# Cosine-weighted linear attention and a mixture of adapters: four rows per partition, Q scaling and V cast on GpSimd, routing in threes

## The chip, the cores and the metric

The kernel runs on one core of one Trainium2 chip. The metric is the device time of one execution in microseconds (us), lower is better. Each run is marked fast, or slow when it lies over 1.5% above the fastest of the same kernel. Medians are of all runs; where kernels are compared, fast runs are compared with fast runs.

Some words that come up: PSUM is where the program's matmuls write, SBUF is where its other tiles lie, and an eviction copies a result from PSUM to SBUF. In the profile's lines PE is TensorE, DVE VectorE, ACT ScalarE and POOL GpSimd; SP issues DMAs.

## The reference, cut to what matters

Eight batches, eight heads, 576 positions, 64 features per head. Attention is linear, so K and V of a batch are first summed into one matrix per head. Its output, 4608 rows of 512, goes through a two-of-eight mixture of rank-16 adapters.

```python
def _attn_ref(q, k, v):                       # (8, 8, 576, 64) each
    theta = np.pi / 2.0 * np.arange(S) / S    # by position
    phi = lambda x: np.concatenate([relu(x) * cos(theta), relu(x) * sin(theta)], axis=-1)
    kv  = einsum('bhsf,bhsd->bhfd', phi(k), v)
    z   = sum(phi(k), axis=2)
    return einsum('bhsf,bhfd->bhsd', phi(q), kv) / (einsum('bhsf,bhf->bhs', phi(q), z) + 1e-6)

def _moe_ref(x, w_gate, A, B):                # x (4608, 512)
    logits = x @ w_gate                       # 8 experts, the two best are taken
    # w = softmax of the two best logits
    # x + sum over the two experts of w_e * (x @ A[e]) @ B[e]
```

## The kernel before

Every batch is cut into five groups of rows, four of 128 and one of 64. Each group loads K, Q and V with a DMA each, in rows of 64 floats, which are 256 bytes. K is scaled on ScalarE, V is cast on ScalarE, Q is scaled on VectorE. TensorE sums K times V over the groups. The attention of a group is eight transposes of Q, an eviction, eight products with `kvzsb`, and a division. The adapters follow, group by group, two groups behind.

```python
for gi, (s0, slen) in enumerate(GROUPS):
    nc.sync.dma_start(out=ks[:slen], in_=k[b, :, s0:s0 + slen, :].transpose([1, 0, 2]))
    nc.sync.dma_start(out=qs[:slen], in_=q[b, :, s0:s0 + slen, :].transpose([1, 0, 2]))
    v_eng.dma_start(out=vs[:slen], in_=v[b, :, s0:s0 + slen, :].transpose([1, 0, 2]))
    # ... K scaled on ScalarE (phi), V cast on ScalarE, 8 matmuls into kvz ...
def attention_back(gi):
    phi_op("vector", qp[:slen, :, 0, :], qs[:slen], cos_tab[:slen, gi:gi + 1])   # and sin
    # ... 8 transposes into qpTp, copied by VectorE into qpT, 8 matmuls into nd ...
    nc.vector.reciprocal(rden[:slen], nd_v[:, :, :, D:W])
    nc.vector.tensor_tensor(out=xt[:slen, :], in0=nd_v[:, :, :, 0:D], in1=rd_rep, op=ALU.mult)
def moe_front(gi):
    # ... 4 transposes of xt, xT copied by VectorE, za = xT @ [A | w_gate] ...
    nc.vector.max(out=m8[:slen], in_=logits)
    nc.scalar.activation(eall[:slen], logits, AF.Exp)
    nc.vector.scalar_tensor_tensor(out=em[:slen], in0=logits, scalar=m8[:slen, 1:2],
        in1=eall[:slen], op0=ALU.is_ge, op1=ALU.mult, accum_out=ssum[:slen])
    nc.vector.reciprocal(rs[:slen], ssum[:slen])
def moe_back(gi):
    # zg = za * rs * em (VectorE), zgT by transpose, dx = xt + zgT @ B (TensorE),
    # osb copied from dx by VectorE and ScalarE in turn
    nc.gpsimd.dma_start(out=out[row0:row0 + slen, :], in_=osb[:slen])
for gi in range(NG + 2):
    # attention_back(gi), moe_front(gi - 1), moe_back(gi - 2)
```

The softmax here doesn't subtract the row's maximum and nothing guards it: scores larger than these inputs give would overflow.

## Time and profile before

| | before |
|---|---|
| median of 3 runs | 198.97 us (196.18 to 202.57) |
| span of the profiled run | 198.0 us |
| TensorE / VectorE / ScalarE / GpSimd busy | 130.2 / 141.6 / 97.6 / 28.6 us |
| DMA packets, of them under 512 B | 120,307, 117,856 |

From the page of the kernel before: busy tenths in 40 equal slices of the span, then the packets, then the DMA queues with packets, megabytes and their share of 16 engines' span.

```profile
DVE  0035557991888889486998399768947799999830
DMA  7999999999999999997999999999999921221121
DMA packets 120307, 38.55 MB, mean 195 GB/s; under 512 B 117856, under 2 KB 117856, under 8 KB 120288
q1 hardware_dynamic: 89216, 21.78, 59.9%
q10 hardware_dynamic: 28128, 7.08, 19.3%
q0 software_dynamic: 2944, 9.44, 13.9%
```

The DMA line stays at nine tenths until about four fifths of the span. Nearly all packets are 256-byte rows. The last eight slices have little DMA work left, while VectorE stays busy: a tail.

The stretches view of the kernel before shows the same by the clock. Columns: the stretch, its length, busy time and instruction count of each engine, the granted TensorE clock, the DMA share, GB/s.

```profile
core 0: us, PE busy (x) PEld busy (x) DVE busy (x) ACT busy (x) POOL busy (x), PEclk, DMA share, GB/s
120.00:150.00 30.00, 22.48 (x235) 14.07 (x235) 22.89 (x84) 16.44 (x34) 5.44 (x16) 0.76 1.11 235
160.00:198.00 38.00, 22.07 (x242) 12.61 (x241) 28.72 (x108) 8.44 (x22) 5.48 (x10) 0.85 0.19 67
```

The DMA share is 1.11 in the first of these stretches (over 1 means that the times of the packets add up to more than 16 engines' time), and VectorE works 28.72 of the last 38 us. The groups of instructions below show what VectorE does for each group of rows (count, then busy us and mean ns of one, then idle time before it; the second line is of the full groups alone).

```profile
L85 DVE TENSOR_SCALAR qp<-qs,cos_tab 128x512 bf16<-128x512 f32 (+1 forms) x40 | 18.8, 470 | 2.5 <-DMA qs<-in_q_dram 2.5
L95 DVE COPY qpT<-qpTp 128x1024 bf16<-128x1024 bf16 x32 | 21.9, 683 | 7.8 <-PE qpTp L185 7.4
```

### The profile page before, as it was taken

Reading aid. Unit: us, or ns where it says so; the run is one execution under the profiler, and the core shown is the slowest. Engines: PE = TensorE matmul, PEld = TensorE weight load, DVE = VectorE, ACT = ScalarE, POOL = GpSimd, SP = SyncE. Lnnn points to the kernel's source line nnn. Section 1 sums busy time; section 2 is a strip of 40 time slices with the busy share of each in tenths; the row PEclk is TensorE's granted clock in tenths of the full one; section 3 lists DMA queues with packets and bytes.
Section 4 is the critical chain, followed back from the end, with each engine's and each line's share of the span. In section 5 each row is a group of like instructions: output and inputs, shape, how many; then the busy total and the mean of one; then the engine's idle time right before and its main releaser. Section 6 shows DMA issues by size and latency. Waiting matters only on the chain. (4 is left out here: it accounts for less than half of the span.)

```text
span 198.0 us, 3992 instructions
## 1 busy us (share of the span) xinstructions
PE 130.2 (66%) x1400; PEld 85.7 (43%) x1400; DVE 141.6 (72%) x503; ACT 97.6 (49%) x193; POOL 28.6 (14%) x87
## 2 busy tenths in 40 slices
PE   0036477782866787589875777589768967776560
PEld 0024356441754455346643455356434655343220
DVE  0035557991888889486998399768947799999830
ACT  0865548564374853548464587365555474201110
POOL 1000000320111121112032012211111302121121
PEclk9999999997578969655999589955975589999855
DMA  7999999999999999997999999999999921221121
GB/s 117 196 218 212 198 220 203 194 281 277 242 188 256 225 294 209 238 277 204 207 234 261 224 192 194 280 227 263 178 259 236 238 63 60 103 79 53 56 106 26
DMA packets 120307, 38.55 MB, mean 195 GB/s; under 512 B 117856, under 2 KB 117856, under 8 KB 120288
## 3 DMA queue, kind: packets, MB, share of 16 engines
q1 hardware_dynamic: 89216, 21.78, 59.9%
q10 hardware_dynamic: 28128, 7.08, 19.3%
q0 software_dynamic: 2944, 9.44, 13.9%
q8 instruction: 11, 0.18, 0.4%
q14 instruction: 8, 0.07, 0.1%
HBM read 28.85 MB, written 9.44 MB: 193 GB/s over the span
## 5 line engine op out<-in xcount | busy, mean ns | idle before, releaser
L297 POOL DMA_DIRECT2D out_dram<-osb x40 | 23.0, 575 | 141.7 <-ACT osb L93 53.3
L160 PE MATMUL kvz<-vsb,kp 128*128 128x65 bf16 (+1 forms) x320 | 22.9, 216 | 21.3 <-ACT kp L81 17.1
L185 PE MATMUL qpTp<-ident,qp 128*128 128x128 bf16 (+1 forms) x320 | 32.8, 252 | 5.9 <-DVE qp L85 5.0
L93 ACT CAST vsb<-vs 128x512 bf16<-128x512 f32 (+1 forms) x40 | 24.2, 616 | 22.2 <-DMA vs<-in_v_dram 22.0
L196 PE MATMUL nd<-kvzsb,qpT 128*128 128x65 bf16 (+1 forms) x320 | 20.9, 217 | 15.6 <-ACT kvzsb L93 8.8
L95 DVE COPY qpT<-qpTp 128x1024 bf16<-128x1024 bf16 (+1 forms) x40 | 25.1, 628 | 7.9 <-PE qpTp L185 7.4
L81 ACT ACTIVATE kp<-ks,cos_tab 128x512 bf16<-128x512 f32 (+1 forms) x40 | 28.7, 719 | 3.5 <-DMA ks<-in_k_dram 3.0
L185 PEld LDWEIGHTS <-qp 128*128 128x128 bf16 (+1 forms) x320 | 23.1, 116 | 16.6 <-DVE qp L85 10.4
L81 ACT ACTIVATE kp<-ks,sin_tab 128x512 bf16<-128x512 f32 (+1 forms) x40 | 28.4, 710 | 2.0 <-DMA ks<-in_k_dram 2.0
L160 PEld LDWEIGHTS <-kp 128*128 128x128 bf16 (+1 forms) x320 | 17.4, 112 | 26.9 <-ACT kp L81 19.1
L248 ACT ACTIVATE eall<-za 128x8 f32<-128x8 f32 (+1 forms) x40 | 6.9, 174 | 42.4 <-DVE m_3115 L246 3.7
L211 DVE TENSOR_TENSOR xt<-nd,rden 128x512 bf16<-128x512 f32 (+1 forms) x40 | 27.1, 678 | 0.0
L196 PEld LDWEIGHTS <-qpT 128*128 128x128 bf16 (+1 forms) x320 | 16.5, 115 | 21.3 <-issue 10.8
L284 PE MATMUL dx<-xt,ident 128*128 128x512 bf16 (+1 forms) x40 | 18.9, 473 | 7.2 <-DVE osb L95 4.1
L286 PE MATMUL dx<-Ball,zgT 128*128 128x512 bf16 (+1 forms) x40 | 19.2, 481 | 6.6 <-DVE zgT L95 6.3
L236 PE MATMUL za<-AW,xT 128*128 128x136 bf16 (+1 forms) x160 | 19.2, 252 | 2.0 <-DVE xT L95 1.5
L85 DVE TENSOR_SCALAR qp<-qs,cos_tab 128x512 bf16<-128x512 f32 (+1 forms) x40 | 18.8, 470 | 2.5 <-DMA qs<-in_q_dram 2.5
L93 ACT COPY osb<-dx 128x512 f32<-128x512 f32 (+1 forms) x20 | 11.6, 581 | 17.7 <-PE dx L286 8.9
L95 DVE COPY xT<-mps 128x512 bf16<-128x512 bf16 (+1 forms) x40 | 15.5, 387 | 4.6 <-PE mps L225 4.4
L225 PE MATMUL mps<-ident,xt 128*128 128x128 bf16 (+1 forms) x160 | 18.1, 242 | 1.1 <-DVE xt L211 0.9
L85 DVE TENSOR_SCALAR qp<-qs,sin_tab 128x512 bf16<-128x512 f32 (+1 forms) x40 | 18.6, 465 | 0.0
L95 DVE COPY osb<-dx 128x512 f32<-128x512 f32 (+1 forms) x20 | 13.6, 682 | 5.2 <-PE dx L286 4.9
(225 smaller groups left out, 116.7 us busy)
## 6 DMA issues: line engine op xcount, KB each, us to landing
ks<-in_k_dram SPq DMA_DIRECT2D x32, 256.0 KB, 6.3
qs<-in_q_dram SPq DMA_DIRECT2D x32, 256.0 KB, 6.0
out_dram<-osb POOLq DMA_DIRECT2D x32, 256.0 KB, 4.7
vs<-in_v_dram ACTq DMA_DIRECT2D x24, 256.0 KB, 5.2
vs<-in_v_dram SPq DMA_DIRECT2D x8, 256.0 KB, 6.8
ks<-in_k_dram SPq DMA_DIRECT2D x8, 128.0 KB, 5.5
qs<-in_q_dram SPq DMA_DIRECT2D x8, 128.0 KB, 5.0
out_dram<-osb POOLq DMA_DIRECT2D x8, 128.0 KB, 3.9
```

Source lines behind the costliest of these rows:

```text
L81: nc.scalar.activation(out_ap, in_ap, func, bias=0.0, scale=scale_ap)
L85: eng.tensor_scalar(out=out_ap, in0=in_ap, scalar1=scale_ap, scalar2=0.0, op0=ALU.mult, op1=ALU.max)
L93: nc.scalar.copy(out_ap, in_ap)
L95: getattr(nc, engine).tensor_copy(out_ap, in_ap)
L160: nc.tensor.matmul(out=kvz[:, gg, j * W:(j + 1) * W], lhsT=kp[:slen, h], rhs=vsb[:slen, h, :], start=(gi == 0 and j == 0), stop=(gi == NG ...
L185: nc.tensor.transpose(out=qpTp[:, h, :slen], in_=qp[:slen, h], identity=ident[:slen, :slen],)
L196: nc.tensor.matmul(out=nd[:slen, gg, j * W:(j + 1) * W], lhsT=qpT[:, h, :slen], rhs=kvzsb[:, h, :], start=True, stop=True,)
L211: nc.vector.tensor_tensor(out=xt[:slen, :], in0=nd_v[:, :, :, 0:D], in1=rd_rep, op=ALU.mult,)
L236: nc.tensor.matmul(out=za[:slen, :], lhsT=xT[:, ci, :slen], rhs=AW[:, ci, :], start=(ci == 0), stop=(ci == DCH - 1),)
L284: nc.tensor.matmul(out=dx[:slen], lhsT=ident[:slen, :slen], rhs=xt[:slen, :], start=True, stop=False)
L286: nc.tensor.matmul(out=dx[:slen], lhsT=zgT[:, :slen], rhs=Ball, start=False, stop=True)
L297: nc.gpsimd.dma_start(out=out[row0:row0 + slen, :], in_=osb[:slen])
```

## The change

The intent is fewer, larger packets, less VectorE work and fewer small routing operations. Row s = 4p + j goes to partition p, so four rows of a head are 1 KB in memory, and a batch's K, V or Q comes with one DMA of 1 MB. The last 64 rows of two batches share a tile, which makes 36 full groups out of 40. GpSimd scales Q and casts V; the ReLU of Q moves into VectorE's eviction. Routing runs once per three groups. The loads of K, V and Q and all stores are issued by SP. The K times V sums of the next batch are spread over the groups of this one.

```diff
-    nc.sync.dma_start(out=ks[:slen], in_=k[b, :, s0:s0 + slen, :].transpose([1, 0, 2]))
+    nc.sync.dma_start(out=t, in_=src[b, :, 0:NP * J, :].rearrange("h (p j) d -> p h (j d)", j=J))
 ...
-    copy_op("act", vsb[:slen, :, 0:D], vs[:slen])
+    nc.gpsimd.tensor_copy(vb[:, :, :, 0:D], main["v", b])
 ...
-    phi_op("vector", qp[:slen, :, 0, :], qs[:slen], cos_tab[:slen, gi:gi + 1])
+    nc.gpsimd.tensor_scalar(out=qp[:, :, i, :], in0=src, scalar1=tab[:, j:j + 1],
+                            scalar2=1.0, op0=ALU.mult, op1=ALU.mult)
 ...
-    copy_op("vector", qpT[:, :, :slen], qpTp[:, :, :slen])
+    nc.vector.tensor_scalar_max(qT, qTp, 0.0)
 ...
-    # per group: max, exp, em (fused, with its sum), rs, zg (fused)
+    # per three groups: 3 max, exp, ge, em = ge * ea, ss, rs, wg = em * rs, zg = za * wg
+    nc.vector.tensor_tensor(out=em, in0=ge, in1=ea, op=ALU.mult)
+    nc.vector.tensor_tensor(out=wg, in0=em, in1=rs.to_broadcast([NP, TRI, E]), op=ALU.mult)
 ...
-    nc.gpsimd.dma_start(out=out[row0:row0 + slen, :], in_=osb[:slen])
+    nc.sync.dma_start(out=dst[:, j, :], in_=osb)      # osb always copied by ScalarE
 ...
-    for gi in range(NG + 2): attention_back(gi); moe_front(gi - 1); moe_back(gi - 2)
+    for u in range(G + 2 * TRI + 1):                  # G = 36
+        k_until(need); q_phi(u); attn(u); k_until(frac)   # k_until: K, V of later batches
+        moe_front(u - 1)
+        if u % TRI == 0: route(u // TRI - 1)
+        finish(u - TRI - 1)
```

## The prediction

> **What bounds the kernel now.** For four fifths of the run, the DMA engines. The page's slices show DMA at nine tenths or more from about 5 to 155 us; the stretches view gives a DMA share of 1.06 to 1.12 between 30 and 150 us. The queue part says why: 117,856 of 120,307 packets are under 512 B (a load row is 64 floats, 256 B). The two hardware queues hold 79.2% of 16 engines' 198 us with 117,344 packets: about 21 ns per packet. VectorE (141.6 us busy) and TensorE (130.2 us) are not saturated then (77% and 73% between 100 and 150 us). After the loads a tail of about 40 us is paced by VectorE: 28.7 of 38 us busy, about 4.4 us per group.
>
> **DMA after.** 512 of 576 rows come in 24,576 packets of 1 KB. [...] Estimates:[...] 12,288 remainder packets at 21 ns = 16 us; stores as now, 13.9% of 198 = 27 us[...]. Sum 113 us instead of about 155. Stores now wait in the SP queue in order with the loads; loads stay about a batch ahead, so I expect little loss.
>
> **VectorE after.** Removed: Q scaling, 37.4 us (80 x 468 ns), and its half of the output evictions, 13.6 us. The ReLU rides in the 1024-wide eviction, 683 ns like the copy. Per full group: 683 + reciprocal 202 + xt 679 + xT 414 = 1.98 us. Routing three groups: about 12 small operations of 150 to 200 ns, zg and the zT copy, some 2.4 us, 0.8 a group. 36 x 2.8 = 100 us. [...]
>
> **ScalarE:** 72 x 715 ns K scaling + 36 x 581 ns evictions + 8 x 588 ns + exps = 83 us.
>
> **GpSimd:** the trace's affine select (128x128, 294 ns) against its memset (128x8, 168 ns) gives about 1.05 ns per element; so 0.7 us for 512 elements, 2.3 us for a V cast: 72 x 0.7 + 8 x 2.3 + 4 x 0.7 = 72 us, an estimate; at twice that it becomes the limit.
>
> **TensorE:** eight transposes take 0.62 us at full clock; about 2 us a group, 75 us, more at a lower clock.
>
> **Critical path.** First K and V arrive as 1 MB each behind the remainders, and K scaling of a batch is 5.7 us: the first attention group starts at about 15 us. Then 36 groups with single-buffered transposes, numerators (the second buffer mostly holds K^T V), za and dx, on in-order engines: about 3.4 us a group (VectorE 80 to 85% busy), 122 us. Final routing and stores: 7 us. Sum 145 us. The limit moves from DMA to a VectorE-centred chain; most of the tail disappears.
>
> Predicted 145 us, 130 to 165. Faster by over 2%: 0.95; within 2%: 0.03; slower: 0.02.
>
> **Right if:** DMA share below 0.9 for most of the run, packets under 512 B near 16,000, GpSimd 60 to 100 us busy, VectorE about 100 us and above 70% of the span, tail under 12 us.
>
> **Wrong if:** GpSimd's scaling takes over 1.3 us each (then GpSimd paces, 160 us and up);[...] stores in the SP queue delay loads; or routing chains stop TensorE[...] and a group costs over 4 us.

Passages that no trace or run of this case shows are cut from it: the time of one 1 KB packet and the DMA term worked out from it, the term for the weights, a wait of VectorE's routing products (in two places), and a clause on the clock. The DMA sum came to 113 us with the two cut terms in it; the terms that are left make 43 us. The 145 us of the critical path loses no term (15 + 122 + 7).

## More of the kernel before

The program states data flow only. When it is built, a scheduler puts the instructions of each engine in one fixed order, and an engine then takes them in that order (in the trace of the change, all 1,324 matmuls, 267 VectorE and 98 GpSimd instructions stand in the built order).

## The result, and the profile after

The change takes 167.4 us (median of 4 runs, 165.15 to 168.39), beside 199.93 us for the kernel before in the same rounds (196.18 to 202.57). The ratio is 0.839, with a 95% interval of 0.81 to 0.868. Ratios are computed as the mean time of one kernel's fast runs over that of the other's fast runs of the same rounds, so they are not quite the ratio of the medians. Results are correct. The profiled run took 168.36 us and counts as slow; the fast ones took 166.44 and 165.15 us at almost the same clock (0.867 and 0.874, against 0.86), and e2_bufs4, which has the same built order (see below), has a fast profile with the same five pauses (7.2 to 13.6 us), so this profile may be read.

The direction is as predicted. The time is 22 us above the predicted 145 and 2 us above the top of the range. Of the prediction's own tests, GpSimd's 67.0 us, VectorE's 93.5 us and the 18,400 small packets come out about as stated. Three do not: the DMA share is 0.91 to 1.14 in every 20 us up to 100 us ("below 0.9 for most of the run"), VectorE is busy 56% of the span ("above 70%"), and the tail after the last `xt` takes 16.7 us ("under 12").

From the page after (first line: busy us and share of the span):

```profile
PE 105.9 (64%) x1324; PEld 78.1 (47%) x1324; DVE 93.5 (56%) x267; ACT 74.4 (45%) x132; POOL 67.0 (40%) x98
DVE  0020065696355988857358728966388369892500
PEclk9999999995987999969569659999597599996955
DMA  5999999996799999948998899569992112221332
DMA packets 47727, 38.50 MB, mean 231 GB/s; under 512 B 18400, under 2 KB 42976, under 8 KB 47712
q1 hardware_dynamic: 42880, 37.75, 75.6%
```

Packets under 512 B fell from 117,856 to 18,400. VectorE is busy 93.5 us, 56% of the span. No engine is busy for more than 64% of the span, and the DMA engines run out of full slices at about three quarters. The stretches view after, columns as before:

```profile
40.00:60.00 20.00, 14.22 (x182) 9.91 (x179) 12.63 (x37) 14.13 (x25) 12.49 (x17) 0.88 0.92 266
80.00:100.00 20.00, 17.00 (x211) 12.72 (x209) 11.43 (x30) 10.95 (x20) 9.14 (x12) 0.68 0.96 291
150.00:167.00 17.00, 7.67 (x38) 3.36 (x37) 3.56 (x14) 3.70 (x7) 0.00 (x0) 0.62 0.27 93
```

VectorE works 12.63 and 11.43 of 20 us in the middle, when the prediction had it 80 to 85% busy. The groups that answer to those shown of before:

```profile
L209 POOL TENSOR_SCALAR qp<-qf,cos_tab 128x512 bf16<-128x512 f32 x32 | 22.1, 692 | 13.3 <-DMA qf<-in_q_dram 7.3
L221 DVE TENSOR_SCALAR qT<-qTp 128x1024 bf16<-128x1024 bf16 x36 | 24.5, 681 | 15.1 <-PE qTp L219 14.9
```

The two Q scalings of a group are now 692 ns each on GpSimd. VectorE pays 681 ns for the eviction with the ReLU, where the 1024-wide copy alone had cost 683 ns.

So the work is as small as expected, but it does not flow. The starts of the 36 `xt` products (one per group, in the timeline of VectorE) come in bursts about 2.3 us apart (median) with five pauses: 13.7 us from 35.8 to 49.5, 10.3 from 70.9, 8.7 from 89.3, 8.5 from 106.6 and 8.9 from 123.6. What happens in the third pause? First the timeline of TensorE after (start us, duration us, engine, line, operation, output and inputs; in brackets the idle time before it and what ended it):

```profile
89.30 0.61 PE L219 MATMUL qTp<-ident,qp 128*128 128x128 bf16 x8
90.85 0.61 PE L219 MATMUL qTp<-ident,qp 128*128 128x128 bf16 x8 [0.53 <-POOL qp L209]
92.59 0.91 PE L219 MATMUL qTp<-ident,qp 128*128 128x128 bf16 x8 [1.14 <-DVE qT L221]
93.52 0.50 PE L292 MATMUL zTp<-ident,zg 128*128 128x128 bf16 x3
94.55 0.58 PE L250 MATMUL xTp<-ident,xt 128*128 128x128 bf16 x4 [0.53 <-DVE zT L294]
94.93 0.63 PE L304 MATMUL dx<-Ball,zT 128*128 128x512 bf16 x1
95.65 0.63 PE L258 MATMUL za<-AW,xT 128*128 128x136 bf16 x4
96.23 0.59 PE L303 MATMUL dx<-xt,ident 128*128 128x512 bf16 x1
96.61 0.65 PE L182 MATMUL kvz<-vb_140,kp 128*128 128x65 bf16 x8
97.07 0.63 PE L227 MATMUL nd<-kvs,qT 128*128 128x65 bf16 x8
```

And VectorE in the same stretch:

```profile
89.89 0.31 DVE L266 MAX8 m_1464<-za 128x8 f32<-128x8 f32 x3
90.12 0.67 DVE L221 TENSOR_SCALAR qT<-qTp 128x1024 bf16<-128x1024 bf16 x1
...
92.91 0.56 DVE L284 TENSOR_TENSOR zg<-za,wg 128x384 bf16<-128x384 f32 x1
...
97.74 0.21 DVE L236 RECIPROCAL rden<-nd 128x8 f32<-128x8 f32 x1 [2.14 <-PE nd L227]
```

At 89.89 the routing of three groups starts with its maxima. TensorE has three groups' Q transposes in its order (89.30, 90.85, 92.59), and then the gate transposes `zTp`, which need `zg`, the end of the routing chain, at 92.91. The numerators `nd` of the next group need only `qT`, evicted at 90.12 to 90.79. They stand after `zTp`, the next `xTp`, two `dx`, `za` and a K times V product, and so start at 97.07. VectorE has nothing for a new group until 97.74. I call a routing *exposed* when no `xt` starts between its maxima and its `zTp`. After the change, seven of twelve routings are exposed, and these seven take 21.7 us from maxima to `zTp`. The five pauses are 50.0 us together, so exposed routings are not the whole of them.

Another view offered a simpler story. In the waits of SP's queue after, stores wait for their evictions, and the loads of the next batches stand behind them in order (in the timeline of SP, the store at 41.21 us had waited 8.2 us, and three loads of 1 MB followed it from 41.61 us):

```profile
SPq L309 <- ACT osb L306: 54.6, 20, 8.2
```

54.6 us of waiting in the queue that issues every load looks like the cause.

### The profile page after: what moved, and what is told of

The parts are those of the page before. It is cut to its first block, busy times and chain, and to the rows that moved or that the text cites. A ratio compares the mean times of both kernels' runs of the same rounds, so it can differ in the third digit from the quotient of the medians.

```text
span 166.6 us, 3415 instructions
## 1 busy us (share of the span) xinstructions
PE 105.9 (64%) x1324; PEld 78.1 (47%) x1324; DVE 93.5 (56%) x267; ACT 74.4 (45%) x132; POOL 67.0 (40%) x98
## 2 busy tenths in 40 slices
DMA packets 47727, 38.50 MB, mean 231 GB/s; under 512 B 18400, under 2 KB 42976, under 8 KB 47712
## 5 line engine op out<-in xcount | busy, mean ns | idle before, releaser
L306 ACT COPY osb<-dx 128x512 f32<-128x512 f32 x36 | 21.0, 584 | 44.8 <-PE dx L304 32.3
L219 PE MATMUL qTp<-ident,qp 128*128 128x128 bf16 x288 | 29.0, 238 | 7.9 <-DVE qT L221 7.2
L221 DVE TENSOR_SCALAR qT<-qTp 128x1024 bf16<-128x1024 bf16 x36 | 24.5, 681 | 15.1 <-PE qTp L219 14.9
L219 PEld LDWEIGHTS <-qp 128*128 128x128 bf16 x288 | 21.4, 107 | 13.6 <-issue 11.3
L209 POOL TENSOR_SCALAR qp<-qf,cos_tab 128x512 bf16<-128x512 f32 x32 | 22.1, 692 | 13.3 <-DMA qf<-in_q_dram 7.3
L182 PEld LDWEIGHTS <-kp 128*128 128x128 bf16 x256 | 15.2, 125 | 22.6 <-ACT kp L154 16.2
L238 DVE TENSOR_TENSOR xt<-nd,rden 128x512 bf16<-128x512 f32 x36 | 24.8, 688 | 0.8
L154 ACT ACTIVATE kp<-kf,cos_tab 128x512 bf16<-128x512 f32 x32 | 22.8, 712 | 5.2 <-DMA kf<-in_k_dram 5.0
L154 ACT ACTIVATE kp<-kf,sin_tab 128x512 bf16<-128x512 f32 x32 | 22.7, 709 | 0.0
L209 POOL TENSOR_SCALAR qp<-qf,sin_tab 128x512 bf16<-128x512 f32 x32 | 22.2, 692 | 0.0
L250 PE MATMUL xTp<-ident,xt 128*128 128x128 bf16 x144 | 16.7, 249 | 4.1 <-DVE zT L294 3.9
L258 PE MATMUL za<-AW,xT 128*128 128x136 bf16 x144 | 16.7, 246 | 1.6 <-DVE xT L253 1.2
L182 PE MATMUL kvz<-vb_136,kp 128*128 128x65 bf16 x96 | 5.6, 214 | 18.8 <-POOL vb_136 L161 17.3
L304 PE MATMUL dx<-Ball,zT 128*128 128x512 bf16 x36 | 16.8, 467 | 0.9 <-DVE zT L294 0.9
```

The lines of the kernel that those rows point to most:

```text
L154: nc.scalar.activation(dst[:, :, i, :], src, AF.Relu, bias=0.0, scale=tab[:, col:col + 1])
L182: nc.tensor.matmul(out=kvz[:, gg, jj * W:(jj + 1) * W], lhsT=lhs(h), rhs=rhs(h), start=(j == 0 and jj == 0), stop=(j == J and jj == 3),)
L209: nc.gpsimd.tensor_scalar(out=qp[:, :, i, :], in0=src, scalar1=tab[:, j:j + 1], scalar2=1.0, op0=ALU.mult, op1=ALU.mult)
L219: nc.tensor.transpose(out=qTp[:, h, :], in_=qp[:, h], identity=ident)
L221: nc.vector.tensor_scalar_max(qT, qTp, 0.0)
L238: nc.vector.tensor_tensor(out=xt, in0=nd_v[:, :, :, 0:D], in1=rden.rearrange("p (g j) -> p g j", g=2).to_broadcast([NP, 2, 4, D]), op=ALU. ...
```

## The experiments

Eighteen kernels ran, each with three rounds; a nineteenth did not build. Medians of the kernel before lie between 198.4 and 200.5 us. In the expectations, A is the theory that stores on SP's queue hold the loads behind them, and B that DMA bandwidth itself is the limit. C is there the theory that single-buffered PSUM chains and the static order set the pace; only in i1_out16 does the letter stand for something else. D comes last. The calls ran on different chips, so a difference of a few us between two calls is not read.

**A warning that applies to all of them.** An edit of one line can make the scheduler reorder the engines. e2_bufs4 and j1_order_kept have the order of the change; every other one that I could compare instruction by instruction differs, and that alone can move the time by some 12 to 15 us (j1_order_kept, below). The differences in time of these runs are then of the edit and of a new order together.

| run | median us (range) | mean of the fast runs (fast of all) | correct | exposed routings of 12, us in them |
|---|---|---|---|---|
| the change | 167.4 (165.15 to 168.39) | 165.8 (2 of 4) | yes | 7, 21.7 |
| e1_stores_act | 154.2 (154.02 to 155.39) | 154.5 (4 of 4) | yes | 3, 10.4 |
| e2_bufs4 | 166.28 (165.49 to 167.92) | 166.5 (4 of 4) | yes | 7, 20.9 |
| e3_prefetch | 165.97 (164.43 to 166.74) | 165.8 (4 of 4) | yes | 2, 4.6 |
| e4_resident | 161.57 (161.12 to 162.45) | 161.7 (4 of 4) | no | |
| e5_tp2 | 167.42 (163.65 to 168.7) | 163.7 (1 of 4) | yes | |
| e6_tri1 | 182.77 (180.59 to 184.68) | 182.0 (3 of 4) | yes | |
| e7_no_gpsimd | 169.61 (168.78 to 171.49) | 169.3 (3 of 4) | yes | |
| e8_layout | 187.37 (186.77 to 188.21) | 187.4 (4 of 4) | yes | |
| f1_resident_nolock | 157.57 (157.01 to 160.06) | 157.5 (5 of 6) | no | |
| f2_resident_split | 153.65 (150.66 to 154.43) | 150.7 (1 of 4) | no | 2, 6.2 |
| f3_act_split | 154.63 (153.12 to 156.08) | 153.4 (2 of 4) | yes | 1, 2.6 |
| f4_all | 155.88 (154.94 to 156.19) | 155.7 (4 of 4) | yes | |
| h1_dma_only | 115.73 (115.04 to 116.7) | 115.8 (4 of 4) | no | |
| h2_stores_pool | 171.62 (170.55 to 173.58) | 171.3 (3 of 4) | yes | 7, 32.3 |
| h3_head | 158.48 (156.74 to 166.05) | 156.9 (2 of 4) | yes | 4, 12.8 |
| h4_all_nolock | 154.5 (153.77 to 158.32) | 154.1 (3 of 5) | yes | |
| i1_out16 | 170.53 (169.51 to 171.68) | 170.6 (4 of 4) | yes | 7, 22.3 |
| j1_order_kept | 170.22 (168.91 to 172.69) | 169.8 (3 of 4) | yes | 7, 23.5 |

The last column was counted in the traces of the runs that the argument needs.

### Stores off SP's queue, more buffers, earlier loads: e1_stores_act, e2_bufs4, e3_prefetch, e4_resident

e1_stores_act issues the stores from ScalarE:

```diff
-            nc.sync.dma_start(out=dst[:, j, :], in_=osb)
+            nc.scalar.dma_start(out=dst[:, j, :], in_=osb)
```

> Only the output stores move from the SP queue to the ScalarE queue, so that loads no longer stand in order behind stores that wait for an eviction. Theory A (loads late because of the stores in the same in-order queue; the SP queue waited 54.6 us for evictions in the changed kernel): the pauses of 8 to 14 us between bursts of attention groups shrink by more than half and the time falls from 166 to 140-152 us. Theory B (the DMA engines are simply full while loads run): within 3% of 166. Theory C (single-buffered PSUM chains and the static order pace it): within 3% of 166.

It took 154.2 us; its runs are 11 us below the fast runs of the change. That seemed to prove A, although the pauses had not halved as A said (below).

e2_bufs4 has four load buffers instead of three (`p_in` bufs 3 to 4, `p_rem` bufs 2 to 3).

> Four load buffers per tensor instead of three (and three remainder buffers instead of two); the order of instructions on every engine is the same as in the changed kernel. If the loads wait for a free buffer (rival to A), the time falls by 5% or more. Under A, B and C it stays within 2% of 166 us; at most the 4.5 us that the SP queue waited for GpSimd's scaling disappears from its waits.

It took 166.28 us: no change, and the order of all instructions is the same as in the change. Load buffers are not the limit. It ran in the same rounds as e1_stores_act and stands 12 us above it.

e3_prefetch puts the loads one batch earlier in the program, with four buffers:

```diff
+    load_kv(1); load_q(1)
 ...
-            if j == 0 and b + 1 < B:
-                load_kv(b + 1); load_q(b + 1)
+            if j == 0 and b + 2 < B:
+                load_kv(b + 2); load_q(b + 2)
```

> Stores stay on the SP queue, but each batch's loads stand one batch earlier in the program (four buffers). Theory A: with a whole batch more of lead the waits behind stores are covered, 142-155 us, and GpSimd's waits for V fall from 42 us to under 20. B and C: within 3% of 166.

It took 165.97 us. SP issued its last load at 101.7 to 106.4 us, earlier than in e1_stores_act (108.3 to 112.7), and nothing was gained. This speaks against A, though the order differs here too. Its longest pause, 15.2 us between two `xt`, has a V cast that waited 6.15 us for its load and one exposed routing in it; what made it I have not settled.

e4_resident loads only batches 0 and 1 and lets the others read the same tiles:

```diff
-            if j == 0 and b + 1 < B:
+            if j == 0 and b + 1 < 2:        # and main[..., b % 2], rem[..., 0] as inputs
```

> Wrong results on purpose: only the first two batches are loaded, batches 2 to 7 compute on their tiles; stores as in the changed kernel. It gives the time of the compute alone with the loads out of the way. A or B: about 20 us until the first group, 36 groups at 2.4 to 2.8 us, 14 us of last chain: 120-135 us. C: 155 us or more.

Without three quarters of the loads it took 161.57 us, only 4 us less than the fast runs of the change and 7 us more than e1_stores_act with all loads. I first concluded that waiting for loads does not separate the change from 154 us. That does not follow, because its order is a new one: from the first Q transposes to the end of the last `xt` it takes 113.7 us (130.0 in the change), and its order then leaves 25.7 us of last chain (16.7 in the change). Whether the missing loads or the new order shortened the first part is not shown. The timeline shows one new stall in this kernel, VectorE's `em` against the run of GpSimd instructions that ended with a V cast:

```profile
36.78 7.87 DVE L274 TENSOR_TENSOR em<-ge,ea 128x24 f32<-128x24 f32 x1
42.73 1.89 POOL L161 CAST vb<-vf 128x2048 bf16<-128x2048 f32 x1
```

`em`, 128x24 elements with both inputs in SBUF, lasted 7.87 us (0.18 us elsewhere). It ended at 44.65 us, when the cast ended at 44.62.

### Undoing one part at a time: e5_tp2, e6_tri1, e7_no_gpsimd, e8_layout

e5_tp2 splits the PSUM bank of `xTp` and `zTp` in two halves, so that transposes need not wait for an eviction.

> The single PSUM buffer that the X transposes and the gate transposes share becomes two halves of the same bank, used in turn. In the last 25 us of the resident run, with no attention work left, a triple took 7.8 us (one group 2.6 us), because transposes, their eviction, the logits, the routing of three and the gate transposes follow one another through single buffers. Theory C (this back-end loop of single buffers paces the kernel, loads or not): 150-161 us. Theory A (late loads alone) or VectorE throughput: within 2% of 166.

167.42 us, with three of four runs slow; the fast one took 163.65 us, 1% below the fast runs of the change. That is no gain that could be told from noise.

e6_tri1 routes each group alone, with the fused operations of before:

```diff
-    TRI = 3
+    TRI = 1
 ...
-        nc.vector.tensor_tensor(out=em, in0=ge, in1=ea, op=ALU.mult)      # and ss, wg
+        nc.vector.scalar_tensor_tensor(out=em[:, 0, :], in0=za[:, 0, ER:ER + E],
+            scalar=m8[:, 0, 1:2], in1=ea[:, 0, :], op0=ALU.is_ge, op1=ALU.mult, accum_out=ss)
```

> Undoes the batching of the routing: per group, with the fused operations of the kernel before; the za bank holds three groups in turn. VectorE has about 0.4 us more work per group, 13 us in all. If VectorE's work counts (as predicted): 172-182 us. Theory C (the batch of three holds za and the transposes for about 3 us of small operations in a row): 150-164 us, with a last chain after the last attention group 5 us shorter.

182.77 us, 16 us slower between fast runs. VectorE is busy 103.1 us, 9.6 more, and there are 36 routing chains instead of twelve; how the 16 us divide between these two and the new order is not shown.

e7_no_gpsimd puts the Q scaling on VectorE and the V cast on ScalarE:

```diff
-            nc.gpsimd.tensor_scalar(out=qp[:, :, i, :], in0=src,
+            nc.vector.tensor_scalar(out=qp[:, :, i, :], in0=src,
 ...
-            nc.gpsimd.tensor_copy(vb[:, :, :, 0:D], main["v", b])
+            nc.scalar.copy(vb[:, :, :, 0:D], main["v", b])
```

> Undoes the move to GpSimd: Q is scaled on VectorE again (72 x 0.47 = 34 us more there), V is cast on ScalarE (about 17 us more there). If VectorE paces: 185-200 us. Theory C (VectorE waits 44% of the time): 165-178 us. Faster than 163 would mean that GpSimd is in the way.

169.61 us, 2% slower between fast runs. VectorE is busy 112.1 us instead of 93.5 and it hardly matters. This speaks against VectorE's work as what paces the change, with the caution that TensorE's order differs from the 136th matmul on.

e8_layout keeps everything but the row order: rows s = 128j + p, four DMAs per tensor and batch.

```diff
-        nc.sync.dma_start(out=t, in_=src[b, :, 0:NP * J, :].rearrange("h (p j) d -> p h (j d)", j=J))
+        for j in range(J):
+            nc.sync.dma_start(out=t[:, :, j, :], in_=src[b, :, NP*j:NP*j+NP, :].transpose([1, 0, 2]))
```

> Undoes the row layout: rows s = 128 j + p, four loads of 256 KB per tensor and batch, in 256 B packets again; everything else as changed. If the packet size is what the change bought: DMA about 155-160 us of loads at 21 ns per packet, 188-202 us in all, close to the kernel before. If the gain came from the engines' share-out instead: 166-175 us.

187.37 us, 22 us slower between fast runs, with the small packets back. From its page:

```profile
DMA  7999999999999999999999999989999999240313
DMA packets 122609, 38.52 MB, mean 207 GB/s; under 512 B 117856, under 2 KB 117856, under 8 KB 122592
```

The DMA slices are full to 85% of the span again. This points to the row order, which makes 1 KB packets, as the larger part of what the change gains over the kernel before. The size of 22 us is not clean, as its instruction order differs too.

### Removing the routing stall and spreading the chain: f1_resident_nolock, f2_resident_split, f3_act_split, f4_all

f1_resident_nolock is e4_resident with `em` made by three fused operations that read the logits from PSUM.

> The resident run again (wrong results on purpose, batches 2 to 7 reuse the tiles of 0 and 1), but the masked exponentials are formed by three fused operations that read the logits from PSUM, so that this step has one SBUF input only. In the resident run one 128x24 product with two SBUF inputs took 7.87 us, until GpSimd's run of back-to-back instructions had ended. [...]

This expectation stood at 150 to 156 us if GpSimd's run held `em`, and at 159 to 163 if it was anything else.

157.57 us. The stall of `em` is gone, and `wg`, the next product of two SBUF inputs, lasted 7.98 us once.

f2_resident_split also puts the gate transposes and everything behind them after the next group's attention (`route` cut in two, its second half called one group later).

> As the run before, and the transposes of the gated activations (with their eviction) are put after the first X transposes of the next triple, so that TensorE does not stand in order behind the routing chain. In the resident run TensorE and its weight loads waited some 18 us for the gate product. Theory C (the serial back-end chain paces): 138-148 us. If the routing chain is hidden by attention work already: within 2% of the run before.

153.65 us; the one run called fast took 150.66. VectorE works 17.68 and 17.59 of 20 us between 40 and 80 us, so with few loads and spread chains it reaches there what the prediction had assumed for the whole kernel.

f3_act_split is e1_stores_act with the same split, with all loads, correct:

```diff
+        tri_zg[t] = zg
+
+    def route_b(t):
+        zg = tri_zg.pop(t)
         zTp = ps_tp.tile([NP, TRI, NP], BF16, name="zTp", tag="tp")
 ...
+        if u % TRI == 1 and 0 <= u // TRI - 1 < G // TRI:
+            route_b(u // TRI - 1)
```

> All loads, correct results: stores on the ScalarE queue (154.2 us) plus the later gate transposes. Theory C: 143-150 us. If with loads the DMA engines pace (B): 151-156 us.

154.63 us: no clear gain over e1_stores_act (fast runs 153.4 against 154.5), although only one routing is exposed.

f4_all adds the loads of K and V of a batch ahead of the 64-row remainders, and the last three outputs on free PSUM banks with evictions on two engines.

> As the run before, and two more things: the main K and V tiles of a batch are loaded ahead of the remainders (first attention group about 3 us earlier), and the last triple's outputs use the free two-bank PSUM buffers and both VectorE and ScalarE (last three evictions, 1.7 us apart now, overlap: about 3 us). 4 to 7 us below the run before: 137-145 us under C, 145-151 us under B.

155.88 us: no gain.

### The floor of the DMA, and the store queue again: h1_dma_only, h2_stores_pool, h3_head, h4_all_nolock

h1_dma_only has all loads and stores of the change and no arithmetic; it stores a constant tile.

> Wrong results on purpose: all loads of the change (same tiles, three buffers, SP queue) and all stores of a constant tile (ScalarE queue), no arithmetic. If DMA is what limits the kernel once the stores are moved (e1_stores_act, 154.2 us, loads there done at about 122 us), the loads alone take about as long as there, 115 to 122 us in all with the stores. If waits of the compute order limit it, the loads alone are done well before, 85 to 105 us in all (estimate: 28.3 MB of main and remainder loads plus 9.4 MB of stores at the 348 GB/s that the stretch from 10 to 20 us of the change shows is 108 us; less if stores overlap better).

115.73 us. From its page:

```profile
DMA  3996999999999999999999999799999999999995
DMA packets 47712, 38.30 MB, mean 333 GB/s; under 512 B 18400, under 2 KB 42976, under 8 KB 47712
```

36 of the 40 DMA slices are at nine tenths or more, so I take this as the floor of this set of transfers. B explains none of the time above 116 us by itself. The prediction's estimate had been 113 us.

h2_stores_pool issues the stores from GpSimd instead (`nc.sync` to `nc.gpsimd` in the two store lines).

> The change with its stores on GpSimd's queue, as before the change, instead of SP's. If the loss is the order of stores ahead of loads on one queue, this recovers about what e1_stores_act did: 152 to 158 us (GpSimd has to issue 40 stores, which also wait for evictions ahead of its scalings, so a few us worse is possible). If the gain of e1 came from something particular to the ScalarE queue, it stays at 165 to 168 us.

171.62 us, slower than the change. Its DMA share is 1.05 to 1.09 from 40 to 100 us, so its loads are early, and that does not help here. GpSimd now waits for the evictions, with Q scalings behind it in order. From the waits view, us in total, times, longest:

```profile
POOL out_dram L309 <- ACT osb L306: 38.3, 17, 5.0
```

VectorE's `em` was long too (5.17 us at 124.56; `em` and `wg` together 17.8 us), and 32.3 us lie in exposed routings. A alone does not account for this: this kernel freed the loads more than e1_stores_act did (see j1_order_kept). But its order is its own, so it is no clean test either.

h3_head is e1_stores_act with K and V of a batch ahead of the remainders, and the weights on GpSimd's queue.

> e1_stores_act with K and V of the first batch issued ahead of the 64-row remainders, and the weights issued on GpSimd's queue. If the head (first attention result at 22.4 us in e1) is simply added to the rest, the first result comes 4 to 5 us earlier and the time is 149 to 151 us. If the loads of the later batches pace the middle, the first result comes earlier but the time stays within 1 us of 154.

158.48 us; its two fast runs took 156.7 and 157.0. The first `xt` came at 23.9 us instead of 22.4: the first Q load is the last of the first batch in both kernels, and Q scaling began at 19.75 us (18.51 in e1_stores_act). The head did not get shorter.

h4_all_nolock adds to h3_head the fused `em`, the split and the banks of f4_all.

> h3_head plus routing through fused operations that read PSUM, the gate transposes deferred by one group, and the last three groups' outputs on the two big PSUM banks with evictions on both engines. Correct results. If head, stalls of the routing products and last chain each add to the rest: 143 to 149 us. If the in-order interleaving and the pace of the loads hold it: 150 to 155 us, no better than e1_stores_act.

154.5 us: no gain over e1_stores_act.

### Queue or order: i1_out16, i2_prefetch_out16, j1_order_kept

In this expectation C is a new rival: stores held behind slow load issues keep the six output buffers full, so that evictions wait and ScalarE and TensorE with them. i1_out16 gives the change 16 output buffers (`p_out` bufs 6 to 16).

> The change with 16 output buffers instead of 6, stores still on the SP queue. Theory A (loads wait behind stores that wait for evictions): more output buffers don't let a load pass a store, so 164 to 168 us. Theory C (stores wait behind load issues, output buffers run out, evictions and with them ScalarE, the single dx bank and TensorE stop): the evictions no longer wait for buffers, 154 to 160 us.

170.53 us: the gain that C forecast is not seen. The test is not clean, because TensorE's order differs from that of the change from the 483rd matmul on; j1_order_kept, where no store stands behind a load in a queue, points the same way. i2_prefetch_out16, e3_prefetch with the 16 buffers, did not fit into SBUF and was not built, so it gave nothing.

> e3_prefetch (loads one batch earlier in the program, four load buffers) with 16 output buffers: neither loads wait for the stores of the batch before nor evictions for buffers. If A and C together are the loss of the SP queue, this reaches e1_stores_act without moving the stores: 152 to 157 us. If something else about the stores on the SP queue costs[...], it stays at 163 to 167 us.

With e1_stores_act, TensorE's order differs from the change from the 262nd matmul on and ScalarE's from the 45th instruction on. D says that this, not the queue, saved the time. j1_order_kept tests it: the stores of e1_stores_act, each right behind its own eviction on ScalarE, and the order of every engine's other instructions pinned to that of the change.

```diff
-            nc.sync.dma_start(out=dst[:, j, :], in_=osb)
+            nc.scalar.dma_start(out=dst[:, j, :], in_=osb)
 ...
+    PINS = {'PE': [172, 173, 174, ...], 'DVE': [...], 'Activation': [...], 'Pool': [...], 'SP': [...]}
+    by_name = {i.name: i for i in nc.cur_bb.bb.instructions}
+    for seq in PINS.values():
+        for a, b in zip(seq, seq[1:]):       # order only, no wait is added
+            tc.add_manual_dep(by_name[f"I-{b}"], f"I-{a}", mybir.DependencyInfo(
+                mybir.DependencyClass.NoSync, mybir.DependencyReason.DATA), reason="pin")
```

> The stores of e1_stores_act (issued by ScalarE, each right after its own eviction), but with the instruction order of TensorE, VectorE, ScalarE and GpSimd pinned to that of the change: the build of e1_stores_act had also reordered TensorE from its 262nd matmul on and ScalarE from its 45th instruction on. Theory A (the queue: loads and stores hold each other on SP): about e1's time, 152 to 157 us. Theory D (the order: moving the stores made the scheduler interleave the engines differently, and that saved the time): no gain over the change, 163 to 168 us. In between: both.

170.22 us. This compares two ways. Against the change, only the queue of the stores differs, and nothing is gained: fast runs take 169.8 us against 165.8. Beside the kernel before in their own rounds the two cannot be told apart (ratios 0.85, 0.839 to 0.861, and 0.839, 0.81 to 0.868). Against e1_stores_act, only the order differs, and the order is worth 15 us between fast runs; with each beside the kernel before in its own rounds it is about 12 us (an estimate from the ratios 0.85 and 0.788 and e1_stores_act's 154.5 us). So moving the stores to another queue is not what saved the time, and D stands. D is also half of the first theory C, which had said that e1_stores_act would gain nothing; it missed because that edit changed the order.

The loads are not free of the stores even here. In the built program loads and stores take turns on the same eight completion semaphores, and a load waits until the DMA before it on its semaphore has landed. From the waits of SP's queue in j1_order_kept, loads (L71, L80) waiting for a store:

```profile
SPq L71 <- DMA out_dram<-osb: 23.0, 3, 7.9
SPq L80 <- DMA out_dram<-osb: 21.2, 7, 6.7
```

That is 44.2 us, and 26.3 us in e1_stores_act; h2_stores_pool, whose stores have semaphores of their own, shows none. The last Q load is issued at 107.9 us in j1_order_kept and at 110.5 in the change, hardly earlier. So j1_order_kept shows that the queue does not matter by itself, but not that late loads cost nothing. e3_prefetch and h2_stores_pool, with earlier loads and no gain, speak against that too, each in an order of its own. Part of what the order of e1_stores_act saves may also come by way of these waits.

The five pauses stay in j1_order_kept. The order of e1_stores_act takes away two of them, and three stay in it:

| us before the | 7th `xt` | 16th | 20th | 25th | 29th | all five | the other 30 gaps |
|---|---|---|---|---|---|---|---|
| the change | 13.7 | 10.3 | 8.7 | 8.5 | 8.9 | 50.0 | 76.6 |
| j1_order_kept | 14.1 | 9.6 | 7.5 | 11.6 | 7.2 | 50.0 | 78.7 |
| e1_stores_act | 14.8 | 9.8 | 3.1 | 11.6 | 3.0 | 42.3 | 70.1 |

The pause before the 20th `xt` is the one shown above.

TensorE in e1_stores_act, at the routing that starts at 84.3 us:

```profile
85.25 0.61 PE L219 MATMUL qTp<-ident,qp 128*128 128x128 bf16 x8 [0.92 <-DVE qT L221]
...
85.94 0.42 PE L227 MATMUL nd<-kvs,qT 128*128 128x65 bf16 x8
...
87.55 0.43 PE L227 MATMUL nd<-kvs,qT 128*128 128x65 bf16 x8
88.01 0.34 PE L292 MATMUL zTp<-ident,zg 128*128 128x128 bf16 x3
```

Two groups' `nd` stand ahead of `zTp`, so the routing chain on VectorE (maxima at 84.30, `zg` at 87.40) runs beside them. TensorE in j1_order_kept, at the routing that starts at 91.9 us:

```profile
93.09 0.61 PE L219 MATMUL qTp<-ident,qp 128*128 128x128 bf16 x8 [0.57 <-DVE qT L221]
94.61 0.61 PE L219 MATMUL qTp<-ident,qp 128*128 128x128 bf16 x8 [0.92 <-DVE qT L221]
95.54 0.34 PE L292 MATMUL zTp<-ident,zg 128*128 128x128 bf16 x3 [0.32 <-DVE zg L284]
...
98.12 0.42 PE L227 MATMUL nd<-kvs,qT 128*128 128x65 bf16 x8
```

Here `zTp` comes first and `nd` 2.6 us behind it; in the change, at the same routing, it was 3.6 us. In the built order of the change and of j1_order_kept, six of the first eleven routings have less than one group's `nd` between the last `za` and `zTp`; in e1_stores_act it is one.

Two cautions. The granted clock went with the order: 0.896 to 0.908 in the runs of e1_stores_act, 0.849 to 0.88 in the fast runs of j1_order_kept. TensorE's busy time is 92.8 against 105.7 us for the same matmuls (16 of the 1,324 matmul records are missing in e1_stores_act). By the table, the pauses make 7.7 us of the difference and the shorter ordinary gaps 8.6; how much the clock had to do with either I have not separated. And e1's order with the stores left on SP was not run, so that the order alone is enough, without moving the stores, is not shown.

## Why the prediction was right or wrong

**The direction and its main cause were right.** Small packets held the kernel before (117,856 of its 120,307 packets). They are down to 18,400, and e8_layout, which brings them back, is the slowest of all runs at 187.37 us (its order is new as well). The estimate of the DMA time, 113 us, met a measured floor of 115.7, but its largest term, that of the 1 KB packets, rested on no run of this case. In h1_dma_only the load queue took 76.1% of 16 engines' 114.9 us; with 12,288 remainder packets at 21 ns, as before, 24,576 packets of 1 KB are left with about 46 ns each (an estimate from these numbers), with the DMA slices as full as shown above.

**The engine sums were right.** Q scaling on GpSimd: 0.7 us predicted, 0.692 measured. V cast: 2.3 predicted, 1.89 measured. GpSimd 67.0 us against 72, VectorE 93.5 against 100, ScalarE 74.4 against 83. Eight Q transposes, 0.62 us in the prediction, took 0.61 us in the change at 90.85 us with a granted clock of 1.00, and 0.91 us at 92.59 us with 0.62 (the first eight, at 19.89 us, took 1.04 us at 1.00).

**The routing products with two SBUF inputs cost about 3 us more.** The prediction allowed for a wait here that no run had shown. In the change, the 24 products `em` and `wg` took 7.4 us instead of 24 times 0.18, which is 4.3: ten that began while GpSimd worked took 0.21 to 0.94 us, the other 14 took 0.17 to 0.18. The longest, `wg` at 68.63 us, ended at 69.57, when a V cast ended at 69.54. It was worse in other orders: `em` lasted 7.87 us in e4_resident, over nine Q scalings and a V cast of GpSimd back to back, and 5.17 us in h2_stores_pool, where `em` and `wg` took 17.8 us together. In f2_resident_split, whose `em` reads the logits from PSUM, the three operations that make `em` took 0.44 to 0.49 us in all twelve routings, while `wg`, with two SBUF inputs, lasted 6.15 us once.

**Moving the stores off SP's queue gained nothing; that their order with the loads costs little, as predicted, is not shown.** The waits view said 54.6 us and e1_stores_act gained 11 us, but j1_order_kept moved the stores alone and gained nothing (169.8 us against 165.8, fast runs), though its loads still waited 44.2 us for stores. h2_stores_pool shows the other side: GpSimd, whose next work is needed, waited 38.3 us for evictions in front of its stores.

**The step that failed is the one on the critical path**: "Then 36 groups with single-buffered transposes, numerators ..., za and dx, on in-order engines: about 3.4 us a group (VectorE 80 to 85% busy), 122 us." Its three terms in the trace after:

| term | predicted us | in the trace of the change |
|---|---|---|
| first attention group starts | 15 | 19.9 (first Q transposes) |
| 36 groups | 122 | 130 (19.9 to 149.9, end of the last `xt`) |
| final routing and stores | 7 | 16.7 (149.9 to the end of the span) |
| sum | 144 (145 stated) | 166.6 |

The middle term is 8 us too small, but its reason is wrong by more than that. It took 3.4 us from VectorE being 80 to 85% busy. VectorE is 56% busy; the groups run about 2.3 us apart and then stop. At two of the five pauses, what stops them is the built order on TensorE, in which the gate transposes of a routing, and what follows them, stand ahead of the next groups' numerators: in the order of e1_stores_act these two fall from 8.7 and 8.9 to 3.1 and 3.0 us, and the middle term is 115.5 us instead of 130. What makes the other three, which stay in both orders, is not settled; in e1_stores_act GpSimd had waited 10.5 us for V by the middle of the second (71.5 us). The prediction named "routing chains stop TensorE" and "a group costs over 4 us" among what would make it wrong; the first of these is this mechanism, at 3.6 us a group, but it was not costed. The built order could have been read before predicting: `nd` counted between `za` and `zTp` shows such places without any time. The count alone does not rank the runs: built again, h3_head has three such routings (158.48 us), h2_stores_pool three (171.62) and e4_resident one (161.57). Every `zTp` that waits for VectorE holds TensorE's stream behind it (8.6 us in seven such waits in the change).

The head was short by 5 us and the last chain by 10, which is the largest miss in the sum. In the head, K landed at 12.3 us, its scaling ended at 17.3 us, and Q scaling began only at 18.5 us, when Q had landed. The last chain is more than the "final routing and stores" of the prediction: the last groups' transposes and `za`, with the three outputs before them, take 5.0 us, the exposed routing 2.3, three outputs through the one `dx` bank 5.5 and the last store 3.9. Neither was bought back: h3_head did not start earlier, and f4_all, whose last chain is 13.8 us against 18.1 in e1_stores_act, did not become faster.

**What stays open.** In a better order the kernel takes 154 us, still 9 above the prediction. By the same three terms e1_stores_act has 19.9, 115.5 and 18.1 us, so the 9 us lie in the head and the last chain; its groups take 3.2 us each, under the predicted 3.4, but not as predicted, for VectorE is 59% busy and three pauses stay. The main loads of e1_stores_act end at about 118 us. By 120 us it has moved 35 of 38.5 MB, which at the mean rate of h1_dma_only (333 GB/s) would take 106 us (an estimate), so DMA leaves it little room. The last batch and its chain take 35 us more. f2_resident_split, with few loads, also needs 153.65 (150.66 in its one fast run). Two limits may lie close together there; none of f3_act_split, f4_all, h3_head and h4_all_nolock, which each attack one or more of them, is below 153. Which one holds is not settled. e3_prefetch, with few exposed routings but 166 us, shows that the count of exposed routings is not the whole of it.

The simplest of the best correct versions that I ran is e1_stores_act, whose fast runs take 154.5 us, 11 us less than those of the change and 42 less than the kernel before in the same rounds. f3_act_split and h4_all_nolock equal it within noise (153.4 and 154.1).

## What to carry to other kernels

When a schedule fixes each engine's order at build time, count what stands between the start of a latency chain and the instruction that waits for it; if no independent work stands there, the whole engine pays the chain, and busy shares will not show it (here 8.6 us of TensorE in seven waits, at a busy share of 64%). An edit that seems to move one queue can reorder other engines (e1_stores_act, some 12 to 15 us), so compare the built orders before believing a gain, and pin the order to test the edit alone. A long wait in a queue (54.6 us here) is a cause only if taking it away, with all else kept, shortens the time; look in the new trace whether the edit did take it away.
